# Channel attention over a cached image: wider running maximum, smaller loads, a short last load and a re-cut of the uncached rows

## The chip, the cores and the metric

The kernel runs on one core of one Trainium2 chip. The metric is the device time in microseconds (us), the median of several executions. The engines are TensorE (PE in the profile; its weight loads are PEld), VectorE (DVE), ScalarE (ACT), GpSimd (POOL) and SyncE (SP). Sixteen DMA engines move data between the device memory (HBM) and the on-chip memory (SBUF), which has 128 partitions. SyncE issues the loads here, ScalarE the stores.

## The reference

The input is one image of 384 x 384 pixels with 96 channels in bf16, 28.3 MB. Every channel gets a scale from its mean and its maximum over all pixels, through two small matrices; then every pixel is multiplied by the scale.

```python
H = W = 384; C = 96; r = 24          # x (1, H, W, C), w1 (C, r), w2 (r, C), all bf16

def reference(x, w1, w2):
    B, H, W, C = x.shape
    xf = x.reshape(B, H * W, C)
    gap = jnp.mean(xf, 1)
    gmp = jnp.amax(xf, 1)
    h_a = gap @ w1
    h_a = h_a * (h_a > 0)            # cast of the comparison left out
    h_m = gmp @ w1
    h_m = h_m * (h_m > 0)
    scale = _sigmoid(h_a @ w2 + h_m @ w2)
    return x * scale[:, None, None, :]
```

So the whole of x has to be seen before the first output can be written.

## The kernel before

The 147,456 pixels are spread over the 128 partitions, 1152 each. In what follows a "row" is one pixel in every partition: 96 values of 2 bytes in each of 128 partitions, 24 KB. A transfer of n rows is 128 contiguous pieces of n x 192 bytes.

SBUF can't hold all 1152 rows. The kernel computes how many fit (NCR, here 1071) and keeps these in a tile named `cache`. The other U = 81 rows are loaded twice: once for the statistics, and once more for the scaling.

```python
RB = 64
ACC_ROWS = 16
...
    acc = small.tile([P, ACC_ROWS, C], BF16, tag="acc")
...
    used = (const.current_size() + small.current_size()) // P
    avail = nc.sbuf_top - nc.sbuf_base
    budget = avail - used - 1024
    NCR = min(NPP, budget // ROWB)
    U = NPP - NCR
```

The first stream loads 64 rows at a time. The uncached rows come first, into slots of the cache that are overwritten by the last loads. VectorE keeps a running maximum in `acc`, 16 rows (1536 elements) per instruction; TensorE adds up the rows by multiplying with a column of ones, five rows (480 columns) per matmul, all into one accumulator.

```python
    for (r0, n, h0) in chunks1:                      # n is 64 for most
        xt = cache[:, h0 : h0 + n, :]
        nc.sync.dma_start(out=xt, in_=xv[:, r0 : r0 + n, :])
        a = 0
        while a < n:
            m = min(ACC_ROWS, n - a)
            if first_dve:
                ...                                  # a copy into acc
            else:
                nc.vector.tensor_tensor(             # L127
                    out=acc[:, 0:m, :], in0=acc[:, 0:m, :],
                    in1=xt[:, a : a + m, :], op=ALU.max)
            a += m
        ...                                          # matmuls into sum_ps, L137
```

Then `acc` is folded from 16 rows to one in four halvings (L150), transposed by TensorE, and reduced over the partitions. The sum takes its own way through ScalarE and ten small matmuls. Both end in two small matmuls and a sigmoid, which leaves `scale` in all 128 partitions.

```python
    rr = ACC_ROWS
    while rr > 1:
        h = rr // 2
        nc.vector.tensor_tensor(out=acc[:, 0:h, :], in0=acc[:, 0:h, :],
                                in1=acc[:, h : 2 * h, :], op=ALU.max)   # L150
        ...
        rr = h
    nc.tensor.transpose(pmaxT_ps[:], acc[:, 0, :], ident[:])
    nc.vector.reduce_max(out=vt[:, 1:2], in_=pmaxT_ps[:], axis=AX.X)
    ...                                              # mean, w1, relu, sum, w2, sigmoid
```

The second stream multiplies 64 rows at a time in place (L184) and stores them (L221). The first 16 uncached rows are reloaded into `acc`, which is free by then; the other 65 go into slots of the cache whose rows have been stored, 64 into that of the first chunk and one into that of the second. They are multiplied LAG = 8 chunks later.

```python
    unc = []
    if U > 0:
        ua = min(U, ACC_ROWS)
        unc.append((NCR, ua, acc[:, 0:ua, :], -1))
        ...                                          # the rest: slots of cache
    LAG = 8
    ...
    if unc and unc[0][3] < 0:
        r0, n, ap, _ = unc[0]
        nc.sync.dma_start(out=ap, in_=xv[:, r0 : r0 + n, :])
        mult(ap, n)
        nc.scalar.dma_start(out=ov[:, r0 : r0 + n, :], in_=ap)
    for ci, (r0, n) in enumerate(chunks2):
        ap = cache[:, r0 : r0 + n, :]
        mult(ap, n)
        nc.scalar.dma_start(out=ov[:, r0 : r0 + n, :], in_=ap)
        ...                                          # reloads, and their multiplies LAG later
```

Of the kernel before, what the change touches and what calls it, by code (L numbers as in the profile page):

```python
# [10 lines left out]
ALU = mybir.AluOpType  # L11
AX = mybir.AxisListType
BF16 = mybir.dt.bfloat16
FP32 = mybir.dt.float32

RB = 64
ACC_ROWS = 16
NEG_BIG = -3.0e38


@with_exitstack
def kernel(
    ctx: ExitStack,
    tc: tile.TileContext,
    x: bass.AP,
    w1: bass.AP,
    w2: bass.AP,
    out: bass.AP,
):
    nc = tc.nc  # L30
    P = nc.NUM_PARTITIONS
    B, H, W, C = x.shape
    Cw, R = w1.shape
    assert Cw == C and tuple(w2.shape) == (R, C)
    assert C <= P and R <= P
    N = B * H * W
    assert N % P == 0, f"{N=} not divisible by {P}"
    NPP = N // P
    ROWB = C * 2

    xv = x.rearrange("b h w c -> (b h w) c").rearrange("(p n) c -> p n c", p=P)
    ov = out.rearrange("b h w c -> (b h w) c").rearrange("(p n) c -> p n c", p=P)

    G = max(1, min(RB, 512 // C))
    MW = G * C

    const = ctx.enter_context(tc.tile_pool(name="const", bufs=1))
    small = ctx.enter_context(tc.tile_pool(name="small", bufs=1))
    psum = ctx.enter_context(tc.tile_pool(name="psum", bufs=1, space=bass.MemoryType.PSUM))

    ones_col = const.tile([P, 1], BF16)
    ident = const.tile([P, P], BF16)
    w1_sb = const.tile([C, R], BF16)
    w2_sb = const.tile([R, C], BF16)
    one11 = const.tile([1, 1], FP32)
    scale = const.tile([P, C], BF16)

    warm = small.tile([P, 1], FP32, tag="warm")
    warm2 = small.tile([P, 1], FP32, tag="warm2")
    acc = small.tile([P, ACC_ROWS, C], BF16, tag="acc")  # L60
    srow = small.tile([1, MW], FP32, tag="srow")
    vt = small.tile([C, 2], BF16, tag="vt")
    hrelu = small.tile([R, 2], BF16, tag="hrelu")
    hp = small.tile([R, P], BF16, tag="hp")

    sum_ps = psum.tile([1, MW], FP32, tag="sum_ps")
    gap_ps = psum.tile([C, 1], FP32, tag="gap_ps")
    pmaxT_ps = psum.tile([C, P], BF16, tag="pmaxT_ps")
    h_ps = psum.tile([R, 2], FP32, tag="h_ps")
    s_ps = psum.tile([P, C], FP32, tag="s_ps")  # L70

    used = (const.current_size() + small.current_size()) // P
    avail = nc.sbuf_top - nc.sbuf_base
    budget = avail - used - 1024
    NCR = min(NPP, budget // ROWB)
    U = NPP - NCR
    assert NCR >= max(U, 1), f"{NCR=} {U=} {RB=} {budget=}"

    cachep = ctx.enter_context(tc.tile_pool(name="cache", bufs=1))
    cache = cachep.tile([P, NCR, C], BF16)  # L80

    nc.vector.memset(warm[:], 0.0)  # L82
    nc.scalar.activation(out=warm2[:], in_=warm[:], func=ACT.Sigmoid)  # L83
    nc.vector.memset(ones_col[:], 1.0)
    nc.vector.memset(one11[:], 1.0)

    nc.scalar.dma_start(out=w1_sb[:], in_=w1)
    nc.scalar.dma_start(out=w2_sb[:], in_=w2)
    masks.make_identity(nc, ident[:])

    chunks1 = []
    if U > 0:
        r = NCR
        while r < NPP:
            n = min(RB, NPP - r)
            chunks1.append((r, n, r - U))
            r += n
    r = 0
    while r < NCR - U:
        n = min(RB, NCR - U - r)  # L100
        chunks1.append((r, n, r))
        r += n
    r = NCR - U
    while r < NCR:
        n = min(RB, NCR - r)
        chunks1.append((r, n, r))
        r += n

    def n_mm(nrows):
        return (nrows + G - 1) // G  # L110

    total_mm = sum(n_mm(n) for (_, n, _) in chunks1)
    mm_i = 0
    first_dve = True
    for (r0, n, h0) in chunks1:
        xt = cache[:, h0 : h0 + n, :]
        nc.sync.dma_start(out=xt, in_=xv[:, r0 : r0 + n, :])
        a = 0
        while a < n:
            m = min(ACC_ROWS, n - a)  # L120
            if first_dve:
                if m < ACC_ROWS:
                    nc.vector.memset(acc[:, m:ACC_ROWS, :], NEG_BIG)
                nc.vector.tensor_copy(out=acc[:, 0:m, :], in_=xt[:, a : a + m, :])  # L124
                first_dve = False
            else:
                nc.vector.tensor_tensor(  # L127
                    out=acc[:, 0:m, :],
                    in0=acc[:, 0:m, :],
                    in1=xt[:, a : a + m, :],  # L130
                    op=ALU.max,
                )
            a += m
        g0 = 0
        while g0 < n:
            g = min(G, n - g0)
            nc.tensor.matmul(  # L137
                sum_ps[:, 0 : g * C],
                ones_col[:],
                xt[:, g0 : g0 + g, :],  # L140
                start=(mm_i == 0),
                stop=(mm_i == total_mm - 1),
            )
            mm_i += 1
            g0 += g

    rr = ACC_ROWS
    while rr > 1:
        h = rr // 2
        nc.vector.tensor_tensor(  # L150
            out=acc[:, 0:h, :], in0=acc[:, 0:h, :], in1=acc[:, h : 2 * h, :], op=ALU.max
        )
        if rr % 2 == 1:
            nc.vector.tensor_tensor(
                out=acc[:, 0:1, :], in0=acc[:, 0:1, :], in1=acc[:, rr - 1 : rr, :], op=ALU.max
            )
        rr = h
    nc.tensor.transpose(pmaxT_ps[:], acc[:, 0, :], ident[:])  # L158
    nc.vector.reduce_max(out=vt[:, 1:2], in_=pmaxT_ps[:], axis=AX.X)  # L159

    nc.scalar.activation(out=srow[:], in_=sum_ps[:], func=ACT.Copy)  # L161
    for g in range(G):
        nc.tensor.matmul(  # L163
            gap_ps[:],
            srow[:, g * C : (g + 1) * C],
            one11[:],
            start=(g == 0),
            stop=(g == G - 1),
        )
    nc.scalar.activation(out=vt[:, 0:1], in_=gap_ps[:], func=ACT.Copy, scale=1.0 / float(N))  # L170

    nc.tensor.matmul(h_ps[:], w1_sb[:], vt[:])  # L172
    nc.scalar.activation(out=hrelu[:], in_=h_ps[:], func=ACT.Relu)  # L173
    nc.vector.tensor_tensor(  # L174
        out=hp[:],
        in0=hrelu[:, 0:1].to_broadcast([R, P]),
        in1=hrelu[:, 1:2].to_broadcast([R, P]),
        op=ALU.add,
    )
    nc.tensor.matmul(s_ps[:], hp[:], w2_sb[:])  # L180
    nc.scalar.activation(out=scale[:], in_=s_ps[:], func=ACT.Sigmoid)  # L181

    def mult(xt_ap, n):
        nc.vector.tensor_tensor(  # L184
            out=xt_ap,
            in0=xt_ap,
            in1=scale[:].unsqueeze(1).to_broadcast([P, n, C]),
            op=ALU.mult,
        )

    chunks2 = []
    r = 0
    while r < NCR:
        n = min(RB, NCR - r)
        chunks2.append((r, n))
        r += n

    unc = []
    if U > 0:
        ua = min(U, ACC_ROWS)  # L200
        unc.append((NCR, ua, acc[:, 0:ua, :], -1))
        r = NCR + ua
        ci = 0
        while r < NPP:
            n = min(RB, NPP - r, chunks2[ci][1])
            unc.append((r, n, cache[:, chunks2[ci][0] : chunks2[ci][0] + n, :], ci))
            r += n
            ci += 1

    LAG = 8  # L210
    pend = sorted([u for u in unc if u[3] >= 0], key=lambda u: u[3])
    loaded = []
    if unc and unc[0][3] < 0:
        r0, n, ap, _ = unc[0]
        nc.sync.dma_start(out=ap, in_=xv[:, r0 : r0 + n, :])
        mult(ap, n)
        nc.scalar.dma_start(out=ov[:, r0 : r0 + n, :], in_=ap)
    for ci, (r0, n) in enumerate(chunks2):
        ap = cache[:, r0 : r0 + n, :]
        mult(ap, n)  # L220
        nc.scalar.dma_start(out=ov[:, r0 : r0 + n, :], in_=ap)  # L221
        for u in pend:
            if u[3] == ci:
                ur0, un, uap, _ = u
                nc.sync.dma_start(out=uap, in_=xv[:, ur0 : ur0 + un, :])
                loaded.append(u)
        while loaded and loaded[0][3] + LAG <= ci:
            ur0, un, uap, _ = loaded.pop(0)
            mult(uap, un)
            nc.scalar.dma_start(out=ov[:, ur0 : ur0 + un, :], in_=uap)  # L230
    for (ur0, un, uap, _) in loaded:
        mult(uap, un)
        nc.scalar.dma_start(out=ov[:, ur0 : ur0 + un, :], in_=uap)


# [28 lines left out]
```

## Time and profile before

The time is 161.49 us, the median of 4 runs (161.39 to 161.53). The profiled span is 159.5 us.

| | busy us | share of span | instructions |
|---|---|---|---|
| PE | 52.7 | 33% | 248 |
| DVE | 130.0 | 82% | 103 |
| ACT | 2.6 | 2% | 6 |
| POOL | 0.7 | 0% | 6 |

The DMA moves 58.67 MB (30.31 MB read, 28.31 MB written), a mean of 368 GB/s over the span.

The page cuts the span into 40 slices of 4.0 us; a digit is the busy share of an engine in that slice, in tenths, and a row gives the GB/s that the DMA moved. A group is all instructions of one line and shape; its row has the count, the busy time, the mean duration of one in ns, and the idle time of its engine just before, with what ended it. In a timeline a row is a stretch of instructions of one line, with its start, its length, and in brackets how long the engine had been idle and what released it.

### The profile page before, as it was taken

The numbers are of one execution on the slowest core, as the hardware profiler recorded it, in microseconds if no ns is written. First come the engines' busy times: TensorE is split into PE (matmuls) and PEld (weight loads), VectorE is DVE, ScalarE is ACT, GpSimd is POOL, SyncE is SP. The second block draws the span as 40 slices with busy tenths as digits, with TensorE's granted clock in tenths as the row PEclk, the third lists the DMA queues.
The fourth block names the chain that finished last, engine by engine and source line by source line (L and its number), as shares of the span: only waits on it lengthen the run. The fifth ranks groups of instructions, "written<-read, shape, count | busy, mean of one in ns | idle before, by whom it ended". The sixth has DMA issues, their size and how long they took to land.

```text
span 159.5 us, 748 instructions
## 1 busy us (share of the span) xinstructions
PE 52.7 (33%) x248; PEld 21.2 (13%) x248; DVE 130.0 (82%) x103; ACT 2.6 (2%) x6; POOL 0.7 (0%) x6
## 2 busy tenths in 40 slices
PE   0298777774777776866010000000000000000000
PEld 0033323231323222323000000000000000000000
DVE  0299999999999999999969999999999999930000
ACT  3000000000000000001010000000000000000000
POOL 1000000000000000000000000000000000000000
PEclk9999999999999999999855555555555555555555
DMA  5999999999999999920034999999999999999995
GB/s 185 412 428 432 428 428 432 422 423 428 425 425 428 418 425 416 437 118 0 0 99 173 419 330 345 416 435 432 425 432 438 419 432 432 422 435 432 425 423 240
DMA packets 6343, 58.67 MB, mean 368 GB/s; under 512 B 1092, under 2 KB 1092, under 8 KB 1732
## 3 DMA queue, kind: packets, MB, share of 16 engines
q1 hardware_dynamic: 3312, 30.30, 46.1%
q10 hardware_dynamic: 3028, 28.32, 42.4%
q8 instruction: 2, 0.03, 0.1%
q14 instruction: 1, 0.01, 0.0%
HBM read 30.31 MB, written 28.31 MB: 368 GB/s over the span
## 4 chain that ended last, share of the span: by engine, by line
DVE 77%; DMA 4%; DVEq 4%; issue 3%; PE 1%; ACT 0%
DVE acc L127 43%; DVE cache L184 32%; DMA cache<-in_x_dram 4%; DVEq L259 4%; DVE acc L150 1%; DVE acc L184 1%; DVE acc L124 0%; PE pmaxT_ps L158 0%; DVE vt L159 0%; DVE hp L174 0%; PE s_ps L180 0%; ACT scale L181 0%; PE h_ps L172 0%; ACT hrelu L173 0%
## 5 line engine op out<-in xcount | busy, mean ns | idle before, releaser
L127 DVE TENSOR_TENSOR acc<-acc,cache 128x1536 bf16<-128x1536 bf16 (+2 forms) x73 | 68.3, 936 | 2.5
L184 DVE TENSOR_TENSOR cache<-cache,scale 128x6144 bf16<-128x6144 bf16 (+2 forms) x19 | 58.3, 3141 | 0.6 <-ACT scale L181 0.6
L137 PE MATMUL sum_ps<-cache,ones_col 128*1 128x480 bf16 (+2 forms) x235 | 50.9, 370 | 22.4 <-DMA cache<-in_x_dram 22.4
L137 PEld LDWEIGHTS <-ones_col 128*1 128x1 bf16 x235 | 20.0, 85 | 52.9 <-issue 27.4
L124 DVE COPY acc<-cache 128x1536 bf16<-128x1536 bf16 x1 | 0.6, 559 | 6.0 <-DMA cache<-in_x_dram 6.0
L158 PE MATMUL pmaxT_ps<-ident,acc 128*96 128x128 bf16 x1 | 0.3, 340 | 5.0 <-DVE acc L150 5.0
L161 ACT ACTIVATE srow<-sum_ps 1x480 f32<-1x480 f32 x1 | 0.6, 560 | 70.7 <-PE sum_ps L137 70.7
L150 DVE TENSOR_TENSOR acc<-acc 128x768 bf16<-128x768 bf16 (+3 forms) x4 | 1.4, 345 | 0.1
L83 ACT ACT_TABLE_LOAD x1 | 1.3, 1283 | 1.2 <-PEq L248 1.2
L163 PE MATMUL gap_ps<-one,srow 1*96 1x1 f32 x10 | 1.0, 220 | 0.7 <-ACT srow L161 0.7
L163 PEld LDWEIGHTS gap_ps<-one,srow 1*96 1x96 f32 x10 | 0.9, 159 | 1.0 <-ACT srow L161 1.0
L184 DVE TENSOR_TENSOR acc<-acc,scale 128x1536 bf16<-128x1536 bf16 x1 | 1.0, 953 | 0.0
L158 PEld LDWEIGHTS <-acc 128*96 128x96 bf16 x1 | 0.2, 153 | 5.1 <-DVE acc L150 5.1
L82 DVE MEMSET warm<- 128x1 f32 x1 | 0.1, 59 | 0.8 <-PEq L248 0.8
L174 DVE TENSOR_TENSOR hp<-hrelu 24x128 bf16<-24x128 bf16 x1 | 0.3, 280 | 0.5 <-ACT hrelu L173 0.5
L159 DVE TENSOR_REDUCE vt<-pmaxT_ps 96x1 bf16<-96x128 bf16 x1 | 0.3, 290 | 0.4 <-PE pmaxT_ps L158 0.4
L180 PE MATMUL s_ps<-w_sb,hp 24*128 24x96 bf16 x1 | 0.3, 257 | 0.6 <-DVE hp L174 0.6
L172 PE MATMUL h_ps<-vt,w_sb 96*24 96x2 bf16 x1 | 0.2, 180 | 0.4 <-DVE vt L159 0.4
masks.py:199 POOL TENSOR_SCALAR_AFFINE_SELECT ident<-ident 128x128 bf16<-128x128 bf16 x1 | 0.3, 292 | 0.1
L181 ACT ACTIVATE scale<-s_ps 128x96 bf16<-128x96 f32 x1 | 0.2, 250 | 0.7 <-PE s_ps L180 0.7
L173 ACT ACTIVATE hrelu<-h_ps 24x2 bf16<-24x2 f32 x1 | 0.2, 161 | 5.7 <-PE h_ps L172 5.7
masks.py:197 POOL MEMSET ident<- 128x128 bf16 x1 | 0.2, 204 | 0.3 <-POOLq L248 0.3
(10 smaller groups left out, 1.1 us busy)
## 6 DMA issues: line engine op xcount, KB each, us to landing
cache<-in_x_dram SPq DMA_DIRECT2D x18, 1536.0 KB, 27.4
out_dram<-cache ACTq DMA_DIRECT2D x17, 1536.0 KB, 13.6
out_dram<-cache ACTq DMA_DIRECT2D x1, 1128.0 KB, 17.4
cache<-in_x_dram SPq DMA_DIRECT2D x2, 408.0 KB, 15.8
cache<-in_x_dram SPq DMA_DIRECT2D x1, 720.0 KB, 27.5
acc<-in_x_dram SPq DMA_DIRECT2D x1, 384.0 KB, 3.2
out_dram<-acc ACTq DMA_DIRECT2D x1, 384.0 KB, 5.3
w_sb<-in_w_dram ACTq DMA_DIRECT2D x2, 4.5 KB, 5.7
```

Of the source, the lines that this page charges most:

```text
L83: nc.scalar.activation(out=warm2[:], in_=warm[:], func=ACT.Sigmoid)
L124: nc.vector.tensor_copy(out=acc[:, 0:m, :], in_=xt[:, a : a + m, :])
L127: nc.vector.tensor_tensor(out=acc[:, 0:m, :], in0=acc[:, 0:m, :], in1=xt[:, a : a + m, :], op=ALU.max,)
L137: nc.tensor.matmul(sum_ps[:, 0 : g * C], ones_col[:], xt[:, g0 : g0 + g, :], start=(mm_i == 0), stop=(mm_i == total_mm - 1),)
L150: nc.vector.tensor_tensor(out=acc[:, 0:h, :], in0=acc[:, 0:h, :], in1=acc[:, h : 2 * h, :], op=ALU.max)
L158: nc.tensor.transpose(pmaxT_ps[:], acc[:, 0, :], ident[:])
L159: nc.vector.reduce_max(out=vt[:, 1:2], in_=pmaxT_ps[:], axis=AX.X)
L161: nc.scalar.activation(out=srow[:], in_=sum_ps[:], func=ACT.Copy)
L163: nc.tensor.matmul(gap_ps[:], srow[:, g * C : (g + 1) * C], one11[:], start=(g == 0), stop=(g == G - 1),)
L174: nc.vector.tensor_tensor(out=hp[:], in0=hrelu[:, 0:1].to_broadcast([R, P]), in1=hrelu[:, 1:2].to_broadcast([R, P]), op=ALU.add,)
L184: nc.vector.tensor_tensor(out=xt_ap, in0=xt_ap, in1=scale[:].unsqueeze(1).to_broadcast([P, n, C]), op=ALU.mult,)
L259: with _tile.TileContext(nc) as tc:
```

## The change

The change works on the time between the end of the loads and the first store, and on the rows that don't fit.

- The running maximum takes 32 rows (3072 elements) per instruction instead of 16, and `acc` is started by a memset with a very small number instead of a copy of the first rows.
- Loads of the first stream have 32 rows instead of 64.
- The first 16 rows of the image are loaded last, as a short load of their own. Ahead of it `acc` is folded from 32 to 16 rows, so that less is left to do once it has landed.
- The margin left free in SBUF is 256 bytes per partition instead of 1024. With the larger `acc` the cache has 1059 rows, and 93 are uncached. Of these 32 are reloaded into `acc` and 61 into the slot of the first chunk; there is no transfer of a single row any more.
- The rows in `acc` are multiplied after the first chunk, and the uncached rows in the cache 6 chunks later instead of 8.
- A path that would give part of the multiply to GpSimd, and one for small first chunks, are written but switched off (P2_POOL_ROWS = 0, FIRST_P2_CHUNKS empty).

The core of the diff:

```diff
 RB = 64
-ACC_ROWS = 16
+RB1 = 32
+ACC_ROWS = 32
+P2_POOL_ROWS = 0
+FIRST_P2_CHUNKS = ()
+TAIL_P1_CHUNK = 16
+LAG = 6
+SBUF_SAFETY = 256
...
-    budget = avail - used - 1024
+    budget = avail - used - SBUF_SAFETY
...
+    nc.vector.memset(acc_d, NEG_BIG)
...
     chunks1 = []
+    tail_rows = min(TAIL_P1_CHUNK, max(0, NCR - U))
+    r = NCR
+    while r < NPP:
+        n = min(RB1, NPP - r)
+        chunks1.append((r, n, r - U))
+        r += n
+    r = tail_rows
     while r < NCR - U:
-        n = min(RB, NCR - U - r)
+        n = min(RB1, NCR - U - r)
         chunks1.append((r, n, r))
         r += n
     r = NCR - U
     while r < NCR:
-        n = min(RB, NCR - r)
+        n = min(RB1, NCR - r)
         chunks1.append((r, n, r))
         r += n
+    if tail_rows > 0:
+        chunks1.append((0, tail_rows, 0))
...
+        if ci == last_ci:
+            while acc_live > max(n, 1) and acc_live % 2 == 0 and acc_live // 2 >= n:
+                h = acc_live // 2
+                nc.vector.tensor_tensor(
+                    out=acc_d[:, 0:h, :], in0=acc_d[:, 0:h, :], in1=acc_d[:, h:acc_live, :], op=ALU.max
+                )
+                acc_live = h
         a = 0
         while a < n:
-            m = min(ACC_ROWS, n - a)
+            m = min(acc_live, n - a)
...
-        ua = min(U, ACC_ROWS)
-        unc.append((NCR, ua, acc[:, 0:ua, :], -1))
+        ua = min(U, acc_rows_total)
+        unc.append(dict(r0=r, n=ua, ap=acc[:, 0:ua, :], after=None))
...
-    LAG = 8
...
     for ci, (r0, n) in enumerate(chunks2):
         ap = cache[:, r0 : r0 + n, :]
         mult(ap, n)
         store(r0, n, ap)
+        if pa is not None and ci == 0:
+            mult(pa["ap"], pa["n"])
+            store(pa["r0"], pa["n"], pa["ap"])
+            pa = None
```

As the changed kernel is built, VectorE's order in the first stream is 33 maxima of 3072 elements and three shorter ones (2784, 2112 and 2784), the fold of 1536, the last maximum of 1536, and a tree of 768, 384, 192 and 96 elements.

## The prediction

> **What bounds the kernel now.** I read the slices of the page first. The kernel has two streams over x, each of 28.3 MB: loads with the maximum and the sum on the way, then the scaling and the stores.
>
> ```profile
> DVE  0299999999999999999969999999999999930000
> DMA  5999999999999999920034999999999999999995
> GB/s 185 412 428 432 428 428 432 422 423 428 425 425 428 418 425 416 437 118 0 0 99 173 419 330 345 416 435 432 425 432 438 419 432 432 422 435 432 425 423 240
> ```
>
> A slice is 4.0 us. VectorE is full throughout both streams, but so is the DMA, at 428 GB/s, with one hole: slices 17 to 21 (counted from 0), about 70 to 86 us. The second stream is limited by DMA alone (VectorE ends four slices before it). So the time is: the loads, the hole, the stores; only a shorter hole, or fewer or faster bytes, can move the end. Next I read the hole in finer stretches (columns: PE, PEld, DVE, ACT, POOL busy with counts, PE clock, DMA share, GB/s).
>
> ```profile
> 69.00:70.00 1.00, 0.17 (x1) 0.08 (x1) 0.96 (x2) 0.00 (x0) 0.00 (x0) 1.00 0.16 56
> 70.00:71.00 1.00, 1.00 (x6) 0.42 (x5) 0.97 (x2) 0.00 (x0) 0.00 (x0) 1.00 0.02 10
> 71.00:72.00 1.00, 1.00 (x7) 0.42 (x5) 0.96 (x2) 0.00 (x0) 0.00 (x0) 1.00 0.00 0
> ```
>
> The last load lands between 70 and 71; the trace's landing records put its last part at 70.76. Then the timeline of the hole (start, length, what):
>
> ```profile
> 63.37 14.99 DVE L127 TENSOR_TENSOR acc<-acc,cache 128x1536 bf16<-128x1536 bf16 x16
> ...
> 69.83 3.44 PE L137 MATMUL sum_ps<-cache,ones_col 128*1 128x480 bf16 x17 [1.39 <-DMA cache<-in_x_dram]
> ...
> 78.40 1.48 DVE L150 TENSOR_TENSOR acc<-acc 128x768 bf16<-128x768 bf16 x4
> ...
> 81.99 3.36 DVE L184 TENSOR_TENSOR cache<-cache,scale 128x6144 bf16<-128x6144 bf16 x1 [0.64 <-ACT scale L181]
> ...
> 85.38 0.38 ACTq L221 DMA_DIRECT2D out_dram<-cache  x1
> ```
>
> VectorE's maximum runs on to 78.38 without a gap, 7.6 us after the last data are there. That is backlog: VectorE is slower than the DMA in the first stream. Then 1.48 us of folding, 2.1 us of small dependent steps, and 3.4 us for the first multiply before the first store. The groups by shape give the cause:
>
> ```profile
> L127 DVE TENSOR_TENSOR acc<-acc,cache 128x1536 bf16<-128x1536 bf16 x70 | 67.1, 958 | 2.4
> ...
> L127 DVE TENSOR_TENSOR acc<-acc,cache 128x1344 bf16<-128x1344 bf16 x1 | 0.9, 857 | 0.0
> ...
> L150 DVE TENSOR_TENSOR acc<-acc 128x768 bf16<-128x768 bf16 x1 | 0.6, 557 | 0.0
> L127 DVE TENSOR_TENSOR acc<-acc,cache 128x96 bf16<-128x96 bf16 x2 | 0.4, 208 | 0.1
> ```
>
> 96 and 1536 elements give (958 - 208) / 1440 = 0.521 ns per element and 158 ns fixed (768 would be 558, the row has 557). Successive starts in the chain of waits lie 0.99 us apart, so some 0.03 us more is lost per instruction. 64 rows take VectorE 4 x 0.99 = 3.97 us; TensorE, which waits for every load, shows them landing every 3.69 us (starts at 46.03, 49.72, 53.40).
>
> [...]no large VectorE memset is in this trace. [...]its packet records have medians of 460 ns for 12,288 B, 220 for 5,760, 128 for 3,264 and 120 for 3,072, so (460 - 120) / 9,216 = 0.0369 ns per byte and 7 ns fixed.
>
> **The change, part by part.**
>
> (1) Wider maximum. One instruction of 3072 elements: 158 + 3072 x 0.521 = 1,758 ns, with the gap 1.78 us per 32 rows, where two of 1536 took 1.98. Over 1152 rows VectorE needs about 64.5 us instead of 71.5.
>
> (2) Smaller loads. A 32-row load is 128 packets of 6,144 B, eight per DMA engine, each 7 + 227 = 233 ns: 1.87 us per load. VectorE's 1.78 is now below it, so VectorE keeps up and the backlog is gone; the first stream becomes DMA-bound. The loads themselves get slightly slower. Before, per DMA engine: 17 x 3.68 + 2 x 1.02 + 1.76 = 66.4 us. After: 33 x 1.87 + 2 x 1.70 (29 rows) + 1.30 (22 rows) + 0.96 (16 rows) = 67.3. So the last load lands 0.9 us later, at about 71.65. [...]
>
> (3) Small last load and early fold. The 29 rows ahead of the last 16 land 0.96 us earlier, at 70.7. VectorE then: 1.63 us for them (72.3), the fold from 32 to 16 rows 0.98 (73.3), the last 16 rows 0.98 (74.3), the remaining tree 1.50 (75.8). The fold is not hidden: the last load lands before VectorE gets to it. TensorE needs about 0.85 us for the last load, then the copy and the ten small matmuls as before, and is done by 75; it does not decide.
>
> (4) The small steps are unchanged: 78.38 + 1.52 = 79.90 to 81.99, 2.1 us. First multiply at 75.8 + 2.1 = 77.9, against 81.99: 4.1 us earlier. The first store follows 3.4 us later as before, at 81.3.
>
> (5) The uncached rows. The larger accumulator costs 16 rows, the smaller margin returns 4: 93 rows are read twice instead of 81. But 32 instead of 16 of them go into the accumulator, in the hole. Work left per DMA engine from the first store on, before: 17 x 3.68 + 2.72 (47 rows) + 1.00 (16) + 3.68 (reload of 64) + 0.24 (one row, twice) = 70.2 us. After: 16 x 3.68 + 3.51 (61 rows stored) + 3.51 (61 reloaded) + 1.87 (32) + 2.04 (35) = 69.8. That is 0.4 us less. The accumulator's reload, 3.2 us for 16 rows before, should take about 4.3 for 32; issued near 76.2 it lands at 80.5, before the first multiply is over at 81.2.
>
> (6) The lag of 6 instead of 8 only reorders VectorE and the stores; VectorE is 16 us ahead at the end, so nothing.
>
> Sum: 4.1 + 0.4 = 4.5 us. 161.49 - 4.5 = 157.0, a ratio of 0.972.
>
> **The rivals.**
>
> *The whole of VectorE's saving arrives.* Taking VectorE's 7.0 us off the end of the maximum puts it near 71.4, and the end near 154.5. The saving would be the whole of the busy time. The last landing at 70.76 speaks against it: with fold, tree and the last rows behind that landing, most of the rest of the hole cannot go away.
>
> *Smaller loads cost bandwidth.* [...]there are 37 loads instead of 20. If each cost a visible fixed 0.1 us, the landing would move by another 2 us, and the result would be 159. Against it: median time from issue to landing is 27.4 us, over seven loads deep, and loads land exactly at the packets' pace (8 x 460 ns = 3.68 against 3.69), so a load's fixed costs are hidden behind the queue. Seven outstanding loads of 1.87 us are still 13 us deep.
>
> *The second stream swallows the gain.* If reloads disturbed the stores more (the page shows 330 and 345 GB/s in the two slices where the reload starts), an earlier start would be partly lost. There is one such start before and one after, so I expect the same dip; a dip doubled would cost some 1.7 us and give 158.7.
>
> *Jitter of the slowest DMA engine.* A load counts only when its slowest engine is done. The landing records show that spread growing from 0.5 to 1.7 us in the load that lands at 38.6, and staying. If the longer program adds another such loss, 1.2 us are gone: 158.2; if none falls there, 155.8.
>
> **Range and chances.** The gain's parts are certain to about half a microsecond each (packet cost, order of the last landings); the DMA's jitter is the largest term, about a microsecond either way. Range: 155.7 to 158.4. Faster by over 2% means below 158.26, which leaves 1.26 us: 0.85. Within 2%: 0.14. Slower by over 2% would need a new wait of 8 us that I see no place for: 0.01.
>
> **What would show it.** In the profile after: groups at 3072 elements with a mean of 1.76 us; VectorE idle before each, released by loads, some 0.08 us; packets of 6,144 B at 233 ns; last load landing near 71.7; last tree step near 75.8; first multiply at 77.9; first store at 81.3; the second stream as long as before less 0.4. I am wrong if VectorE still has no gaps in the first stream (its 1.78 was too low), if loads land more than 1.9 us apart, or if the second multiply waits for the accumulator's reload.

## The result and the profile after

The changed kernel takes 156.72 us (median of 8 runs, 156.46 to 157.39) against 161.55 us for the kernel before (13 runs). The ratio is 0.970, with a 95% interval of 0.969 to 0.972. The profiled span went from 159.5 to 155.1 us.

First the slices of the page after; a slice is now 3.9 us, so they no longer line up exactly with those of before.

```profile
DVE  6799999959999998999779999999999999940000
DMA  5999999999999999991066999999999999999995
GB/s 159 421 422 423 425 417 418 418 415 415 421 415 420 417 415 421 414 413 45 0 203 269 390 372 430 425 434 428 428 426 436 428 434 428 434 425 437 425 427 213
```

The hole in the DMA row is still there, but shorter. In the full slices of the first stream the DMA moves a mean of 418 GB/s (413 to 425, slices 1 to 17) where it was 425 (412 to 432, slices 1 to 16): this is the price of the smaller loads. Finer stretches show the end of the loads (columns: PE, PEld, DVE, ACT, POOL, PE clock, DMA share, GB/s).

```profile
70.00:71.00 1.00, 0.98 (x6) 0.34 (x5) 1.00 (x1) 0.00 (x0) 0.00 (x0) 1.00 0.23 92
71.00:72.00 1.00, 0.81 (x5) 0.34 (x5) 0.97 (x2) 0.00 (x0) 0.00 (x0) 1.00 0.08 31
72.00:73.00 1.00, 1.00 (x7) 0.41 (x5) 1.00 (x1) 0.00 (x0) 0.00 (x0) 1.00 0.00 0
```

The landing records put the last part of the last load at 72.09. The timeline of the hole:

```profile
59.42 13.65 DVE L144 TENSOR_TENSOR acc<-acc,cache 128x3072 bf16<-128x3072 bf16 x8 [0.56 <-DMA cache<-in_x_dram]
...
71.19 1.99 PE L154 MATMUL sum_ps<-cache,ones_col 128*1 128x480 bf16 x10 [0.21 <-DMA cache<-in_x_dram]
...
73.11 0.96 DVE L137 TENSOR_TENSOR acc<-acc 128x1536 bf16<-128x1536 bf16 x1
...
74.10 0.96 DVE L144 TENSOR_TENSOR acc<-acc,cache 128x1536 bf16<-128x1536 bf16 x1
...
75.09 1.49 DVE L167 TENSOR_TENSOR acc<-acc 128x768 bf16<-128x768 bf16 x4
...
78.68 3.36 DVE L204 TENSOR_TENSOR cache<-cache,scale 128x6144 bf16<-128x6144 bf16 x1 [0.63 <-ACT scale L198]
81.95 1.75 DVE L204 TENSOR_TENSOR acc<-acc,scale 128x3072 bf16<-128x3072 bf16 x1
82.07 0.38 ACTq L219 DMA_DIRECT2D out_dram<-cache  x1
```

The maxima of the large loads now end at 73.07, one microsecond after the last landing, where 7.6 us passed before. VectorE now waits for data: up to 57.10 its maxima start 1.88 us apart, with some 0.12 us idle before each, but for one wait of 1.55 us up to 34.49, for the load that lands at 34.39. The 0.56 us before 59.42 are another thing. The row puts them down to a load, but that load had landed at 58.91, and the chain of waits has 0.46 us there in which the engine waited for nothing that the profile shows:

```profile
43.84 15.08 DMA cache<-in_x_dram
...
58.96 0.46 issue
59.42 1.77 DVE acc L144
```

From there on VectorE is behind the loads and waits for none of them up to the end of the maximum. What held it is not looked into here. That the loads bound most of the first stream now is also seen in the page's summary of this chain (the work that ended last, followed back, by engine): DMA's share of it rose from 4% to 36%, and VectorE's fell from 77% to 45%. Before and after:

```profile
DVE 77%; DMA 4%; DVEq 4%; issue 3%; PE 1%; ACT 0%
```

```profile
DVE 45%; DMA 36%; issue 3%; DVEq 2%; SPq 1%; PE 1%; ACT 0%
```

The groups by shape have the mean of the wide maximum at 1,758 ns, the number that was predicted, and the memset at 2,618.

```profile
L144 DVE TENSOR_TENSOR acc<-acc,cache 128x3072 bf16<-128x3072 bf16 x33 | 58.0, 1758 | 6.3 <-DMA cache<-in_x_dram 3.0
...
L97 DVE MEMSET acc<- 128x3072 bf16 x1 | 2.6, 2618 | 0.6 <-issue 0.6
```

So the 4.35 us by which the span shrank come in two parts. The first multiply starts at 78.68 instead of 81.99: 3.31 us. The stretch from the issue of the first store to the landing of the last one is 71.97 us (82.07 to 154.04) instead of 73.07 (85.38 to 158.45): 1.10 us. (Together 4.41; the span ends 0.06 us later behind the last landing. The difference of the medians is 4.83: the profiled execution of the changed kernel, at 156.89 us, was 0.17 slower than the median, and some 0.25 us lies outside the profiled span and is not looked into here.)

### The profile page after: what moved, and what is told of

The parts are those of the page before. It is cut to its first block, busy times and chain, and to the rows that moved or that the text cites. A ratio compares the mean times of both kernels' runs of the same rounds, so it can differ in the third digit from the quotient of the medians.

```text
span 155.1 us, 779 instructions
## 1 busy us (share of the span) xinstructions
PE 55.1 (36%) x265; PEld 22.5 (15%) x265; DVE 128.1 (83%) x67; ACT 2.6 (2%) x6; POOL 0.7 (0%) x6
## 2 busy tenths in 40 slices
DMA packets 8503, 58.96 MB, mean 380 GB/s; under 512 B 1076, under 2 KB 1076, under 8 KB 6196
## 4 chain that ended last, share of the span: by engine, by line
DVE 45%; DMA 36%; issue 3%; DVEq 2%; SPq 1%; PE 1%; ACT 0%
DMA cache<-in_x_dram 36%; DVE cache L204 33%; DVE acc L144 9%; DVEq L303 2%; SPq L133 1%; DVE acc L204 1%; DVE acc L167 1%; DVE acc L137 1%; PE pmaxT_ps L175 0%; DVE vt L176 0%; DVE hp L191 0%; PE s_ps L197 0%; ACT scale L198 0%; PE h_ps L189 0%; ACT hrelu L190 0%
## 5 line engine op out<-in xcount | busy, mean ns | idle before, releaser
L144 DVE TENSOR_TENSOR acc<-acc,cache 128x3072 bf16<-128x3072 bf16 (+3 forms) x37 | 63.4, 1715 | 6.5 <-DMA cache<-in_x_dram 3.0
L154 PE MATMUL sum_ps<-cache,ones_col 128*1 128x480 bf16 (+1 forms) x252 | 53.4, 354 | 19.8 <-DMA cache<-in_x_dram 19.7
L204 DVE TENSOR_TENSOR cache<-cache,scale 128x6144 bf16<-128x6144 bf16 (+2 forms) x18 | 57.4, 3263 | 0.6 <-ACT scale L198 0.6
L154 PEld LDWEIGHTS <-ones_col 128*1 128x1 bf16 x252 | 21.3, 84 | 51.6 <-issue 25.9
L97 DVE MEMSET acc<- 128x3072 bf16 x1 | 2.6, 2618 | 0.6 <-issue 0.6
L204 DVE TENSOR_TENSOR acc<-acc,scale 128x3072 bf16<-128x3072 bf16 x1 | 1.8, 1751 | 0.0
L137 DVE TENSOR_TENSOR acc<-acc 128x1536 bf16<-128x1536 bf16 x1 | 1.0, 957 | 0.0
## 6 DMA issues: line engine op xcount, KB each, us to landing
cache<-in_x_dram SPq DMA_DIRECT2D x33, 768.0 KB, 15.1
```

The costliest lines, as they stand in the source:

```text
L97: nc.vector.memset(acc_d, NEG_BIG)
L137: nc.vector.tensor_tensor(out=acc_d[:, 0:h, :], in0=acc_d[:, 0:h, :], in1=acc_d[:, h:acc_live, :], op=ALU.max)
L144: nc.vector.tensor_tensor(out=acc_d[:, 0:m, :], in0=acc_d[:, 0:m, :], in1=xt[:, a : a + m, :], op=ALU.max,)
L154: nc.tensor.matmul(sum_ps[:, 0 : g * C], ones_col[:], xt[:, g0 : g0 + g, :], start=(mm_i == 0), stop=(mm_i == total_mm - 1),)
L204: nc.vector.tensor_tensor(out=xt_ap[:, 0:ndve, :], in0=xt_ap[:, 0:ndve, :], in1=scale[:].unsqueeze(1).to_broadcast([P, ndve, C]), op=ALU.mult,
```

## The experiments

Each has its own runs of the kernel before on the same chip; times are medians, in brackets the ratio to that kernel with its 95% interval. The edits are shortened to the lines that matter.

### What each half of the first stream's change brings

```diff
 # kernel before                     # wide_max_only
-ACC_ROWS = 16
+ACC_ROWS = 32
```

> The kernel before with one change: the running maximum takes 32 rows per instruction; loads stay at 64 rows, no short last load, old second stream (97 rows uncached, of which one is reloaded alone). Theory (the backlog of VectorE was the hole, and wide instructions alone remove it): VectorE needs about 3.56 us per 64 rows against 3.69 between landings, so it has idle gaps; last 64 rows land near 68.9 and the last 33 near 70.8, so maxima end near 74.5, the five-level tree near 77.0, first multiply at 79.1 (before 81.99, after 78.68); time about 158 to 158.5. Rival (the smaller loads bring the gain): less than 1 us is gained, 160.5 or more.

Measured: 157.80 us (0.977, 0.976 to 0.979). The timeline:

```profile
68.92 5.59 DVE L127 TENSOR_TENSOR acc<-acc,cache 128x3072 bf16<-128x3072 bf16 x4 [0.15 <-DMA cache<-in_x_dram]
74.54 2.48 DVE L150 TENSOR_TENSOR acc<-acc 128x1536 bf16<-128x1536 bf16 x5
...
79.03 3.36 DVE L184 TENSOR_TENSOR cache<-cache,scale 128x6144 bf16<-128x6144 bf16 x1 [0.63 <-ACT scale L181]
```

The first multiply is within 0.1 us of the theory. One constant moves it by 2.96 us, most of the 3.31 of the whole change. The last load lands at 70.70 here, 1.4 us earlier than with loads of 32 rows: the loads of 64 rows were the cheaper ones here. But VectorE gets its last rows in larger lumps and ends 3.8 us after that landing, where the changed kernel takes 1.0. So the smaller loads bring only the last 0.35 us of the first multiply's gain. (The constant also changes the second stream: 97 rows are uncached here, and 32 of them are reloaded into `acc`.)

```diff
 # kernel before                     # small_loads_only: in the first stream
-    n = min(RB, ...)
+    n = min(RB1, ...)               # RB1 = 32
```

> The kernel before with one change: loads of the first stream have 32 rows instead of 64; maximum still 16 rows per instruction. Theory: VectorE stays the bound of the first stream (1.98 us per 32 rows against 1.87 for a load), but starts near 5.0 instead of 6.94, so its maxima end near 76.8 instead of 78.38; time about 160.0. Rival (smaller loads are what matters): as the changed kernel, 157. Second rival (smaller loads cost bandwidth): no gain or a loss, 161.5 or more.

Measured: 160.06 us (0.991, 0.990 to 0.992), again by the theory. VectorE works on without a gap and has its backlog at the end, 4.6 us after the last landing (72.15):

```profile
57.78 18.97 DVE L128 TENSOR_TENSOR acc<-acc,cache 128x1536 bf16<-128x1536 bf16 x20
76.78 1.49 DVE L151 TENSOR_TENSOR acc<-acc 128x768 bf16<-128x768 bf16 x4
```

What it gains (first multiply at 80.37 instead of 81.99) is VectorE's earlier start: its first instruction on a load begins at 5.17 instead of 6.94.

### The short last load

```diff
 # kernel after                      # no_short_tail
-TAIL_P1_CHUNK = 16
+TAIL_P1_CHUNK = 0
```

> The changed kernel without the short last load and its early fold: the last load has 29 rows, the tree has five levels. Theory (the fold was not hidden, because VectorE has no spare time before the last landing): last landing near 72.1 as in the changed kernel, maximum of 29 rows to 73.8, tree 0.98 + 1.49, end of tree at 76.2 against 76.58; time 156.4, that is 0.3 us faster or the same. Rival (the short tail hides the fold): 1 us slower, 157.7.

Measured: 156.93 us (0.971, 0.970 to 0.973), which cannot be told from the changed kernel. The timeline has the first multiply 0.2 us earlier than with the short load.

```profile
59.22 14.65 DVE L144 TENSOR_TENSOR acc<-acc,cache 128x3072 bf16<-128x3072 bf16 x9 [0.54 <-DMA cache<-in_x_dram]
73.90 2.48 DVE L167 TENSOR_TENSOR acc<-acc 128x1536 bf16<-128x1536 bf16 x5
...
78.48 3.36 DVE L204 TENSOR_TENSOR cache<-cache,scale 128x6144 bf16<-128x6144 bf16 x1 [0.63 <-ACT scale L198]
```

The short load with its early fold brings nothing. It was meant to hide the fold, but VectorE has no spare time there in which to hide it: it runs from 59.22 to the end of the tree with gaps of 0.04 us at most.

### Why the last landing is late: an instruction fetch

```diff
 # kernel after                      # fewer_matmuls (leaves out most matmuls of the sum)
-        while g0 < n:
+        while g0 < n and (ci < 10 or ci == last_ci):
```

> The changed kernel with the matmuls of the sum left out for all loads but the first ten and the last (the mean is then wrong; loads, maxima, stores are all there). TensorE's program falls from about 510 to under 200 instructions. In the traces of both kernels two packets of 16,384 bytes on an instruction queue take 1.07 us each, and after the first of them the spread between the first and the last DMA engine of a load goes from 0.4 to 1.9 us and stays. Theory (the fetch of TensorE's program holds up one DMA engine, and the last landing waits for that engine): the two packets are gone, the spread stays near 0.4, the last load lands at about 70.6 instead of 72.1, the time falls by 1.2 to 1.5 us, to 155.3. Rival (the spread has another cause, or another engine's program is fetched): spread and time unchanged, 156.7.

Measured: 155.98 us (0.966, 0.965 to 0.967). The pages before and after both have this line among their DMA queues (packets, MB, share):

```profile
q8 instruction: 2, 0.03, 0.1%
```

All queues of this run (q1 has the loads, q10 the stores):

```profile
q1 hardware_dynamic: 5616, 30.60, 48.8%
q10 hardware_dynamic: 2884, 28.32, 43.8%
q14 instruction: 1, 0.01, 0.0%
```

The two fetches are gone, and with them the long spread: in the landing records the first and the last DMA engine of a load are 0.4 us apart up to 61 us, where the changed kernel has 1.8 to 1.9 from 34 us on. There the first fetch starts at 31.19, and in the load that is then under way 15 engines land within 0.4 us (by 32.96) and one at 34.39. The last load lands at 71.33 instead of 72.09. That is 0.76 us, not the 1.2 to 1.5 expected, because near 61 us another fetch, of 8,192 bytes on q14, raises the spread to 1.0. That fetch is in the changed kernel too, where the larger spread is there already: of the 16 engines of its last load 13 are done by 70.66, and the other three at 71.27, 72.06 and 72.09. So the fetches of TensorE's program cost the changed kernel about 0.75 us. (The run also leaves out what TensorE reads from SBUF; that this has no part in it is argued from the moment at which the spread jumps.)

### The second stream: why 1.10 us and not 0.4

The work on the DMA engines explains 0.4 us. The rest must be time that they lose. Stretches of both traces around the reload of uncached rows into the cache, of before and then of after, show it; the last column is GB/s, and 429 is the rate of the later stores in both.

```profile
93.40:99.50 6.10, 0.00 (x0) 0.00 (x0) 6.10 (x3) 0.00 (x0) 0.00 (x0) 0.50 0.97 304
```

```profile
88.50:90.60 2.10, 0.00 (x0) 0.00 (x0) 2.10 (x2) 0.00 (x0) 0.00 (x0) 0.50 0.99 291
```

When the reload starts, packets of 12,288 bytes take up to 950 ns instead of 460. Before, this costs 6.1 x (1 - 304/429) = 1.8 us; after, 0.7. These sums are rough: with the 0.4 us of work they would make 1.5 us, where 1.10 was measured. Some expectations below count the loss in another way, with larger figures. The packet records show one more difference. Before, the stores have a hole from 94.97 to 97.70: 68 packets of the reload start in it, of up to 989 ns, and none with data of a store, though one had been issued at 92.79. After, packets of both queues go on side by side from 89.6 on. Four runs were made to find what sets this.

```diff
 # kernel before                     # no_single_row
-    budget = avail - used - 1024
+    budget = avail - used - 832
```

> The kernel before with a margin of 832 instead of 1024 bytes: 80 rows uncached instead of 81, so 16 + 64 and no transfer of a single row; also two maxima of 96 elements fewer (0.46 us of VectorE in the first stream, which is its bound). Theory (the second reload, of one row, makes its own disturbance in the stores): the stretch from the first store to the last landing is 73.07 in the kernel before; it shrinks by 0.24 for the row itself and by about 0.7 more, to 72.1; time 161.55 - 0.46 - 0.95 = 160.1. Rival (the single row costs only its packets): the stretch is 72.8, time 160.85.

Measured: 161.00 us (0.997, 0.996 to 0.998); first store to last landing 73.04 us. The stretch did not change: the single row costs it nothing. Of the 0.6 us gained the trace shows 0.28 in the earlier first store (85.10), somewhat less than the 0.46 reckoned for the two short maxima; some 0.2 lies outside the profiled span.

```diff
 # kernel before                     # late_reload
-        ci = 0                       # chunk behind which the reload is issued
+        ci = 4
```

> The kernel before with the reload of the 64 uncached rows put behind the fifth chunk instead of the first, and that of the single row behind the sixth. Work and first stream unchanged. Theory (the stretch from the first store to the last landing is 1 us shorter in the changed kernel because the reload meets a store queue with more work waiting, thanks to the larger accumulator's store): VectorE's lead is larger by then, so the stretch shrinks from 73.1 to about 72.1; time 160.6. Rival (the joining of loads and stores costs the same whenever it happens): stretch 73.1, time 161.5.

Measured: 160.93 us (0.996, 0.995 to 0.998); first store to last landing 72.57 us, which is half of the gain expected. The loss is 4.0 x (1 - 313/429) = 1.1 us: later is somewhat cheaper in this one run.

```diff
 # kernel after                      # small_acc_reload
-        ua = min(U, acc_rows_total)
+        ua = min(U, 16)
```

> The changed kernel, but only 16 of the 93 uncached rows reloaded into the accumulator; the other 77 go into slots of the cache as 64 and 13. Work per DMA engine from the first store on rises by 1.0 us (70.8 instead of 69.8). Theory (the larger accumulator store is what shortens the stretch beyond its work): stretch from first store to last landing 70.8 + 2.9 = 73.7, time 158.5. Rival (only the work counts): 70.8 + 2.2 = 73.0, time 157.7.

Measured: 159.00 us (0.984, 0.982 to 0.986); first store to last landing 73.81 us (82.07 to 155.88), as the theory has it; the time is 0.5 us longer than it said. Of the 1.84 us that the stretch gains, 1.0 is work. The slow time at the reload is long again:

```profile
90.00:96.50 6.50, 0.00 (x0) 0.00 (x0) 6.50 (x3) 0.00 (x0) 0.00 (x0) 0.50 1.01 325
```

In these runs the loss goes with the size of the accumulator's reload and store: with 32 rows, in the kernel after, in wide_max_only, no_short_tail and fewer_matmuls, the stretch from first store to last landing is 71.9 to 72.1 us; with 16, in the kernel before, small_loads_only and no_single_row, it is 73.0 to 73.2. That the size itself decides is not shown, for something else changes with it. With 32 rows VectorE's multiply of them takes 0.8 us longer, so the next store is issued later, and the reload, which waits for the landing of the first chunk, follows it more closely. Before and after:

```profile
89.52 0.34 ACTq L221 DMA_DIRECT2D out_dram<-cache  x1
90.60 6.21 SPq L225 DMA_DIRECT2D cache<-in_x_dram  x2
```

```profile
87.00 0.34 ACTq L219 DMA_DIRECT2D out_dram<-cache  x1
87.25 0.33 SPq L266 DMA_DIRECT2D cache<-in_x_dram  x1
```

The reload is issued 0.24 to 0.27 us behind a store in those four runs with 32 rows, and 1.04 to 1.08 us behind one in those three with 16 and in small_acc_reload. late_reload, with 16 rows, has 0.53 us, a loss in between and no hole in its stores over 0.7 us. So the place of the reload behind the store is a rival that no run here separates from the size. The next run asked for the mechanism.

```diff
 # kernel before                     # small_packets_at_reload: second stream
-        n = min(RB, NCR - r)
+        n = min(32 if 64 <= r < 128 else RB, NCR - r)
```

> The kernel before with one change: rows 64 to 127 of the second stream are multiplied and stored as two chunks of 32 rows (packets of 6,144 bytes) instead of one of 64 (12,288 bytes). These are the stores that the 64-row reload meets when it is issued. Bytes unchanged. Theory (the reload's packets wait for about ten store packets on each DMA engine, and the engine loses time in proportion; 10 x 460 ns against 10 x 234 ns, as the 4.7 and 2.3 us from issue to first packet in the runs so far): first reload packet 2.3 us after issue, about 1 us less lost, stretch from first store to last landing 72.1 instead of 73.07, time about 160.6. Rival (the size of the accumulator's store counts, not the packets met): first packet 4.7 us after issue, stretch 73.1, time 161.5.

Measured: 161.52 us (1.000, 0.999 to 1.001). The first reload packet still comes 4.9 us after the issue (90.51 to 95.42), and the loss is the long one:

```profile
93.50:99.00 5.50, 0.00 (x0) 0.00 (x0) 5.50 (x2) 0.00 (x0) 0.00 (x0) 0.50 1.02 303
```

The packets met were indeed of 6,144 bytes, and took about 450 ns instead of 234. The size of the packets met is not the mechanism; that theory falls.

### Trying for a better version

```diff
 # kernel after                      # small_first_stores
-TAIL_P1_CHUNK = 16
+TAIL_P1_CHUNK = 0
-FIRST_P2_CHUNKS = ()
+FIRST_P2_CHUNKS = (32,) * 6
-        if pa is not None and ci == 0:
+        if pa is not None and ci == 1:
```

> The changed kernel without the short last load, with the first six chunks of the second stream at 32 rows, and the accumulator's rows multiplied after the second of them. Theory (the end follows the first store, as long as VectorE keeps ahead of the stores): the first store is issued 1.75 us after the first multiply instead of 3.36; VectorE needs 1.78 us per 32 rows against 1.87 for their store, so no gap opens; first store 1.6 us earlier, time about 155.2. Rival (VectorE is hardly faster than the stores, so the early start only opens gaps later): 156.5 to 157.

Measured: 156.58 us (0.969, 0.968 to 0.971). The first store is issued at 80.32, 1.75 us before that of the changed kernel, but the last landing is only 0.26 us earlier. The rival's result, but not its reason: the DMA is busy from 81 us on, at a slightly lower rate, and then loses time at the reload, 6.6 x (1 - 310/429) = 1.8 us, with a hole of 3.5 us in the stores. The accumulator holds 32 rows here too, so its size alone does not make the loss short.

```profile
81.00:100.40 19.40, 0.00 (x0) 0.00 (x0) 19.40 (x10) 0.00 (x0) 0.00 (x0) 0.50 1.01 416
100.40:107.00 6.60, 0.00 (x0) 0.00 (x0) 6.60 (x3) 0.00 (x0) 0.00 (x0) 0.50 1.00 310
```

Three more runs build on this one: the reload early among small packets, then in addition loads of 64 rows for the first part of the first stream, then in addition the reload in the stores' own queue.

```diff
 # small_first_stores                # early_small_reload: into the first two slots
-            unc.append(dict(r0=r, n=n, ap=cache[:, cr0 : cr0 + n, :], after=ci))
+            unc.append(dict(r0=r, n=n, ap=cache[:, 0:n, :], after=2))
```

> The changed kernel without the short last load, with the first six chunks of the second stream at 32 rows as in the run of small first stores, but with the 61 rows reloaded into the slots of the first two chunks, behind the third chunk, so that the reload meets store packets of 6,144 bytes. Theory (in the run of small first stores the earlier start was eaten by a costlier reload: 2.3 us lost on the DMA engines against 1.0): the loss falls back to 1.0, the earlier first store comes through, time about 155.2. Rival (the early start is lost because VectorE cannot keep ahead of the stores): 156.5.

Measured: 157.05 us (0.972, 0.970 to 0.973). Again against the theory: the loss moves to the earlier place and stays, 8.1 x (1 - 341/429) = 1.7 us.

```profile
86.40:94.50 8.10, 0.00 (x0) 0.00 (x0) 8.10 (x5) 0.00 (x0) 0.00 (x0) 0.50 1.00 341
```

```diff
 # early_small_reload                # mixed_loads
-        n = min(RB1, NCR - U - r)
+        n = min(64 if r < 448 else RB1, NCR - U - r)
```

> As the run with the early reload among small packets, and the loads of the first 448 cached rows are 64 rows each; the later ones 32. Theory (each extra load of 32 rows costs 0.05 us of packet overhead and 0.02 us between loads): the last landing is about 0.5 us earlier, and VectorE still ends right behind it, since eighteen small loads follow; 0.4 us faster than that run, 154.8. Rival (the last landing is set by the held-up DMA engine alone, or VectorE's backlog from the large loads does not vanish): no difference.

Measured: 156.29 us (0.967, 0.966 to 0.968), that is 0.8 us faster than the run before it. The last load lands at 71.62 instead of 72.15, as expected; the first multiply comes 0.47 us earlier. The time stays 1.5 us above the 154.8 expected, which rested on a small loss at the reload; that is still 7.6 x (1 - 349/429) = 1.4 us.

```diff
 # mixed_loads                       # reload_on_store_queue
-            ..., after=2))
+            ..., after=5))
-                nc.sync.dma_start(out=u["ap"], ...)
+                nc.scalar.dma_start(out=u["ap"], ...)
```

> The kernel of the run with mixed loads, with the reload of the 61 rows issued by ScalarE behind the sixth store, so that it stands in one queue with the stores instead of joining them from SyncE's queue. Bytes unchanged. In the runs so far the DMA engines lose 1.0 to 2.7 us around this reload, and neither the single row nor the packet size explains how much. Theory (the loss comes from a second queue joining a busy one): most of the loss of 2.5 us goes, the stretch from first to last store packet falls from 72.4 to about 70.5, time about 154.5. Rival (the loss comes from reading among writes, or from the start of a read, in whatever queue): time 156.3 as before.

Measured: 155.86 us (0.964, 0.963 to 0.966). It is the fastest kernel that computes everything, 0.6% faster than the change, but not by the theory: the loss is still there, 7.0 x (1 - 316/429) = 1.8 us.

```profile
92.50:99.50 7.00, 0.00 (x0) 0.00 (x0) 7.00 (x3) 0.00 (x0) 0.00 (x0) 0.50 1.00 316
```

So it is not two queues meeting either. A loss of 0.5 to 1.8 us where the reload starts among the stores is seen in each of the eleven traces in which it was reckoned; what decides between the short and the long loss stays open. The last four runs have the reload 0.35 to 1.92 us behind a store, 32 rows in the accumulator and losses of 1.4 to 1.8 us, so neither the size nor the distance accounts for all of them. A run without any reload, which needs a kernel that leaves rows out, wasn't made.

## Why the prediction was right, point by point

The time was 157.0 predicted and 156.7 measured. The terms:

| step | predicted | measured |
|---|---|---|
| (1) maximum of 3072 elements | 1,758 ns | 1,758 ns |
| (2) time between landings, 32 rows | 1.87 us | 1.88 us |
| (2) last landing | 71.65 | 72.09 |
| (3) maxima of the large loads end | 72.3 | 73.07 |
| (3) tree ends | 75.8 | 76.58 |
| (4) first multiply | 77.9 | 78.68 |
| (4) first store | 81.3 | 82.07 |
| (5) first store to last landing | 0.4 less | 1.10 less |

**Bound.** The mechanism was right: VectorE's backlog was the hole, the wide instruction removes most of it, and the first stream becomes DMA-bound, with 0.12 us idle before VectorE's maxima where 0.08 were predicted. The run with the wide maximum alone shows it by itself.

**The first part of the sum was 0.8 us too large** (4.1 against 3.31). Of this, 0.44 us is the last landing. The loads' packets of 6,144 bytes have a median of 236 ns, where 233 was predicted, and landings are 1.88 us apart and not 1.87; over 36 intervals this is the half microsecond. I had said that a load's fixed costs are hidden behind the queue; eight packets of 236 ns are 1.89 us, so none is seen. (The terms of step (2) as printed also add up to 67.4 us, not 67.3.) The other 0.3 us is a wait that step (3) of the prediction left out: it let VectorE begin the 29-row load ahead of the last as it landed. That load landed at 71.14, and VectorE began it at 71.47. Two things make this up. The last loads land 1.82, 1.66 and 0.95 us apart (the last two are shorter loads), and VectorE still had the one before, 1.78 us for 32 rows, to finish; that alone is an estimated 0.16 us (landed at 69.48, started at 69.52, done at 71.30, had VectorE been on time). The rest is left of the 0.46 us that VectorE lost at 58.96 and had only partly made up.

**The second part was 0.7 us too small** (0.4 against 1.10). I counted work, and expected the same dip at the reload. The dip is smaller: 0.7 us lost instead of 1.8. It goes with the larger reload into the accumulator, by two groups of runs and small_acc_reload, but whether by its size or by the moment of the next store is open.

The two errors nearly cancel in the time, so the total is better than its parts. That is luck: without the smaller dip, which was not foreseen, the time would have been an estimated 157.4 (156.7 + 0.7), still inside the range.

**The short last load.** The prediction said that the fold is not hidden; it did not draw the conclusion that the short load is then worth nothing. The experiment did.

**Rivals.** "The whole of VectorE's saving arrives" fell as argued: of its 7.0 us, 3.31 reached the first multiply, for the last landing stood in the way. "Smaller loads cost bandwidth" was right in kind and small: 1.4 us of the last landing in all (70.70 with large loads in wide_max_only, 72.09 here), of which 0.9 had been reckoned, and half a microsecond in mixed_loads for fourteen small loads joined into seven. Loads of 768 KB moved 418 GB/s where those of 1.5 MB moved 425, so the smaller ones cost under 2% of the rate. That was with about eight loads queued (15.1 us from issue to landing, 1.88 us apart); a shorter queue was not tried. "The slowest DMA engine" is real: the spread of 1.7 to 1.9 us is in both kernels, and now has a cause, the instruction fetches. It was about the same in both, so it hardly moved the difference between them. "The second stream swallows the gain" did not happen to the change, but it is what happened to small_first_stores. The memset, whose length no trace of the kernel before shows, took 2.62 us and was over at 4.15, before the first load landed at 4.95; VectorE then sat idle for 0.90 us until that load (its first maximum starts at 5.05), so the memset cost nothing.

## What to carry to other kernels

When two engines that work one behind the other are both nearly full, compare their time per piece (here 3.97 and 3.69 us per 64 rows): the slower one's backlog at the end of the stream is the time to gain, and no more than down to the faster one's last landing. A fold or a small last piece ahead of that landing brought nothing here, because the engine had no idle time there. And check what an earlier start triggers before counting it: the DMA gave back 1.5 us of a store issued 1.75 us sooner.

## What was not expected of the hardware

- An instruction fetch of 16,384 bytes took 1.07 us on a DMA engine, and from the load then under way one engine landed late: the spread of landings went from 0.4 to 1.8 us and was 1.8 to 1.9 in every later load of the stream. With the fetches gone, the last landing is 0.76 us earlier.
- Where the reload started among stores in full flow, their packets of 12,288 bytes took about 900 ns instead of 460 for some 2 us (93.8 to 95.9 before, 88.6 to 90.5 after), and 0.5 to 1.8 us were lost in all in the eleven traces reckoned. The loss was also there (1.8 us) when the load stood in the same queue as the stores. In six of the runs with the long loss the stores then paused for 2.3 to 3.5 us while the load alone went on.
